# The w1_out product of a fused attention and MoE kernel by one Strassen level over groups of four token tiles, with the order of all engines written out

## The chip, the cores and the metric

One core of one Trainium2 chip. The time is the device time of one execution in microseconds (us), lower is better. Before the change three runs took 1277.09, 1277.37 and 1279.2 us; the median is 1277.37.

TensorE (PE) multiplies; "PEld" is its weight load. VectorE (DVE), ScalarE (ACT) and GpSimd (POOL) do the rest, SyncE (SP) issues the DMA transfers. SBUF is the on-chip memory, PSUM the banks that TensorE writes, DRAM the memory outside.

## The reference

Three parts follow each other for 4608 tokens of 512 numbers.

```
# attention: q, k, v of 8 batches x 8 heads x 576 tokens x 64; k and v averaged over 8 tokens each
scores = scale * q @ k_pooled.T;  attn = softmax(scores);  x = attn @ v_pooled      # x: 4608 x 512

# layer 1: w_in 512 x 1024, g_ln 1024, w_out 1024 x 512
h    = x @ w_in
solu = h * softmax(h)
ln   = (solu - mean(solu)) / sqrt(var(solu) + 1e-6) * g_ln
x    = ln @ w_out                  # the product that the change is about

# layer 2: w_in 512 x 2048, w_out 2048 x 512
h = x @ w_in;  x = (h * sigmoid(h)) @ w_out
```

## The kernel before, in words

Every product is computed to float32 accuracy from pairs of a high part and a low part: a number x is split into hi, a rounded copy, and lo = x - hi, and a product takes three matmuls (hi x hi, hi x lo, lo x hi). The splitting is work for the other engines: ScalarE copies (L181), VectorE subtracts (L182).

The 4608 tokens are 36 tiles of 128. Attention and layer 1 make up the first stage (0 to 582.49 us of the profiled execution). Per tile they run scores (`sp`, L403), softmax (L420, with GpSimd scaling the probabilities into `pb` at L429 and `lf` at L435), transposes of the probabilities (`pm` L454, `pl` L459), the product with the values (`av`, L505), the hidden product of layer 1 (`hp`, L534), its maximum (L545), the exponent (L552), the product with it (L553), a square with the sum (L562) and the scaling to the normed row on GpSimd (`e`, L568). `norm_T` transposes a normed tile (`tp`, L582) and splits it into `ln`.

`project1` multiplies by w1_out (`w1oh` and `w1ol`, scaled by g). It works on groups of two tiles (GT = 2, 256 tokens), in four chunks of 128 output columns: for each of 8 blocks of the inner dimension one 512-wide matmul (the high weights against high and low parts of `ln` side by side, L597) and one 256-wide (the low weights against the high parts, L598). ScalarE copies one half of the result (L601), VectorE adds the other (L602), and a DMA writes it to `x2d` in DRAM.

Beside this run the conversions of the weights, which lie in DRAM as pairs of 32-bit words: `tail` (L201 on ScalarE, or L205 on VectorE) and a bit join (L206). The second stage, from 582.49 us, is layer 2: its first product (L834) and its last (L1075), both by one Strassen level already.

The order of TensorE's instructions in the first stage is written by hand: SCRIPT up to tile 35, STEP and TAIL after it. A word stands for a piece (S scores, X softmax, T transposes, a or A the product with the values, H hidden product, M, E, Z the parts of the norm, N `norm_T`, P one chunk of `project1`, B a piece of the background work, W matmuls that only keep TensorE busy). `manual_schedule` holds TensorE to this order; the instructions of the other engines are put in order by a scheduler.

```
            nc.tensor.matmul(xp, wide["w1oh"][:, k, cs], ln[:, k], start=(k == 0), stop=False)
            nc.tensor.matmul(
                xp[:, :GW], wide["w1ol"][:, k, cs], ln[:, k, 0], start=False, stop=(k == FC1 - 1)
            )
        nc.scalar.activation(xo, xp[:, :GW], AF.Copy)
        nc.vector.tensor_tensor(xo, xp[:, GW:], xo, op=ALU.add)
```

## Time and profile before

| | us |
|---|---|
| runs | 1277.09, 1277.37, 1279.2 |
| span of the profiled execution | 1274.6 |
| the profiled execution's own time: its span and what lies around it (1277.37 - 1274.6 = 2.8, by the median run) | 1277.4 |
| TensorE busy | 1247.3 (98%) |
| VectorE busy | 893.1 (70%) |
| ScalarE busy | 785.8 (62%) |
| GpSimd busy | 341.7 (27%) |

The span runs from the first to the last instruction in the trace; what the execution takes beyond it lies around it. A busy share is an average over the whole span, and the two stages differ, so the rows further down are cut by stage. A row of windows has its stretch, its length, the busy us (and instruction count) of PE, PEld, DVE, ACT and POOL, the granted TensorE clock as a share of full speed, the DMA share and the GB/s moved. Each matmul line has two numbers: the busy time, in which overlapping instructions count once, and the mean duration of one, in which the pipelined part of a matmul counts too; their product is more than the busy time.

### The profile page before, as it was taken

The page shows a single profiled execution, that of the slowest core. Times are in us where ns is not written, and L with a number is a line of the kernel's source. Part 1 is how long each engine was busy: PE and PEld are TensorE (multiplying, and loading weights), DVE is VectorE, ACT ScalarE, POOL GpSimd, SP SyncE. Part 2 cuts the span into 40 slices and gives each one's busy share as a digit, 9 for nine tenths or more (in the row PEclk, how much of TensorE's full clock was granted, in tenths as well). Part 3 has the DMA queues.
Part 4 walks back from the last instruction along what each step waited for, and adds up shares of the span by engine and source line. Part 5 has one row for each costly group of instructions (what it writes and reads, how often), then busy time and mean ns, then how long its engine had stood idle before and what let it go on. Part 6 is the DMA issues. An engine that isn't in the chain of part 4 may idle for free.

```text
span 1274.6 us, 20717 instructions
## 1 busy us (share of the span) xinstructions
PE 1247.3 (98%) x6916; PEld 1124.7 (88%) x6916; DVE 893.1 (70%) x1481; ACT 785.8 (62%) x2009; POOL 341.7 (27%) x519
## 2 busy tenths in 40 slices
PE   5799999999999999999999999999999999999998
PEld 4688888888888888889999999999987888888888
DVE  6896577766765555565767676666479987969776
ACT  7975657566666566446677677667635545554544
POOL 3444344334343333332424333332040000000000
PEclk8899999999999999999999999999999999999999
DMA  8754155533533212034777697675999888777683
GB/s 295 253 188 146 54 163 167 172 123 126 171 107 124 84 62 75 26 135 144 285 288 257 242 350 284 242 247 211 366 350 395 321 285 279 268 265 259 198 294 135
DMA packets 118858, 268.76 MB, mean 211 GB/s; under 512 B 11456, under 2 KB 50368, under 8 KB 117216
## 3 DMA queue, kind: packets, MB, share of 16 engines
q1 hardware_dynamic: 118752, 267.44, 60.4%
q8 instruction: 55, 0.90, 0.3%
q14 instruction: 51, 0.42, 0.1%
HBM read 183.50 MB, written 83.89 MB: 210 GB/s over the span
## 4 chain that ended last, share of the span: by engine, by line
PE 91%; DVE 4%; ACT 3%; DMA 1%; issue 1%; POOL 0%; SPq 0%; DVEq 0%
PE m L834 27%; PE op L1075 25%; PE hp L534 14%; PE xp L597 10%; PE xp L598 5%; PE sp L403 3%; PE av L505 2%; PE tp L582 2%; PE pm L454 1%; ACT pr L420 1%; DVE gr L618 1%; DMA early<-w1i 1%; DVE gt L618 1%; PE pl L459 0%; ACT tail L201 0%
## 5 line engine op out<-in xcount | busy, mean ns | idle before, releaser
L834 PE MATMUL m<-t,w2s 128*128 128x384 f32 x2016 | 350.1, 334 | 0.0
L834 PEld LDWEIGHTS m<-t,w2s 128*128 128x128 f32 x2016 | 349.3, 188 | 0.4 <-DVE xo L602 0.3
L1075 PE MATMUL op<-gt,w2o 128*128 128x512 f32 (+1 forms) x1680 | 346.2, 368 | 0.4 <-DVE gt L618 0.3
L1075 PEld LDWEIGHTS op<-gt,w2o 128*128 128x128 f32 x1680 | 292.5, 189 | 54.1 <-DVE gt L618 2.0
L1055 ACT ACTIVATE gt<-gr 128x512 fp32r<-128x512 f32 (+1 forms) x240 | 139.8, 588 | 144.1 <-DVE gt L618 56.5
L597 PE MATMUL xp<-ln,w1oh 128*128 128x512 f32 x576 | 206.2, 399 | 0.5 <-DVE ln L182 0.4
L618 DVE TENSOR_TENSOR gt<-gr,gt 128x512 fp32r<-128x512 f32 (+1 forms) x240 | 155.1, 652 | 61.7 <-ACT gt L1055 58.3
L598 PE MATMUL xp<-ln,w1ol 128*128 128x256 f32 x576 | 161.1, 280 | 0.0
L597 PEld LDWEIGHTS xp<-ln,w1oh 128*128 128x128 f32 x576 | 108.2, 188 | 23.5 <-DVE ln L182 0.6
L534 PE MATMUL hp<-w1ih,xTh 128*128 128x512 f32 x288 | 116.5, 404 | 2.8 <-DVE e L553 2.1
L420 ACT ACTIVATE pr<-sp,st 128x72 f32<-128x72 f32 x288 | 89.3, 333 | 47.3 <-DVE st L412 46.1
L534 PE MATMUL hp<-w1ih,xTl 128*128 128x512 f32 x288 | 113.0, 392 | 0.4 <-DVE xTl L182 0.4
L534 PE MATMUL hp<-w1il,xTh 128*128 128x512 f32 x288 | 112.4, 390 | 0.0
L598 PEld LDWEIGHTS xp<-ln,w1ol 128*128 128x128 f32 x576 | 108.4, 188 | 0.4
L618 DVE TENSOR_TENSOR gr<-gr 128x512 f32<-128x512 f32 (+1 forms) x120 | 79.9, 668 | 0.2
L429 POOL TENSOR_TENSOR pb<-pr,st 128x512 f32<-128x512 f32 x36 | 38.0, 1054 | 136.8 <-DVE st L426 134.9
L545 DVE TENSOR_REDUCE ls<-hp 128x1 f32<-128x1024 f32 x36 | 44.0, 1222 | 37.5 <-PE hp L534 37.3
L618 POOL TENSOR_TENSOR tt<-x2r 128x768 f32<-128x768 f32 x22 | 43.6, 1982 | 96.4 <-DMA x2r<-x2d 67.9
L181 ACT ACTIVATE ln<-tp 128x512 fp32r<-128x512 f32 x72 | 39.6, 599 | 44.0 <-PE tp L582 43.8
L534 PEld LDWEIGHTS hp<-w1ih,xTh 128*128 128x128 f32 x288 | 54.2, 188 | 14.0 <-DVE e L553 2.7
L534 PEld LDWEIGHTS hp<-w1ih,xTl 128*128 128x128 f32 x288 | 54.0, 188 | 12.9 <-DVE xTl L182 1.0
L420 ACT ACTIVATION_READ_ACCUMULATOR pr<-sp,st 128x1 f32 x288 | 62.9, 219 | 0.0
(135 smaller groups left out, 1965.0 us busy)
## 6 DMA issues: line engine op xcount, KB each, us to landing
w2o<-wod SPq DMA_DIRECT2D x50, 768.0 KB, 6.2
x2r<-x2d SPq DMA_DIRECT2D x12, 1536.0 KB, 7.5
gd<-ga SPq DMA_DIRECT2D x96, 192.0 KB, 2.3
gd<-gb SPq DMA_DIRECT2D x48, 384.0 KB, 2.7
w2o<-wod SPq DMA_DIRECT2D x33, 512.0 KB, 6.0
gr<-gd SPq DMA_DIRECT2D x31, 512.0 KB, 7.2
wod<-wo SPq DMA_DIRECT2D x56, 256.0 KB, 2.5
gr<-gd SPq DMA_DIRECT2D x55, 256.0 KB, 5.7
```

Source lines behind the costliest of these rows:

```text
L181: nc.scalar.activation(hi, src, AF.Copy)
L403: nc.tensor.matmul(sp[done : done + n, p // 2, (p % 2) * 2 * SP : (p % 2 + 1) * 2 * SP], q[:, p, done : done + n], kbd[b % 2][:, p, :], st ...
L420: nc.scalar.activation(pr[:, g, h], sv[:, g, h], AF.Exp, bias=st[:, 0, g, h : h + 1], accum_out=st[:, 1, g, h : h + 1],)
L429: nc.gpsimd.tensor_tensor(pb, pr[:, :, :, 0:64], st[:, 0].rearrange("p a (h o) -> p a h o", o=1).to_broadcast([P, 2, 4, 64]), op=ALU.mult,)
L534: nc.tensor.matmul(hp[:, f], l, r, start=(n == 1 and m == 0), stop=(n == KC and m == 2))
L545: nc.vector.tensor_reduce(nm, hp.rearrange("p a n -> p (a n)"), axis=AX, op=ALU.max, negate=True)
L597: nc.tensor.matmul(xp, wide["w1oh"][:, k, cs], ln[:, k], start=(k == 0), stop=False)
L598: nc.tensor.matmul(xp[:, :GW], wide["w1ol"][:, k, cs], ln[:, k, 0], start=False, stop=(k == FC1 - 1))
L618: eng.tensor_tensor(dst, a, b, op=ALU.subtract)
L834: nc.tensor.matmul(to, wt[:, a, o : o + P], tk[:, b, k], start=(start and k == 0 and m == 0), stop=(k == 1 and m == 2), skip_group_check=n ...
L1055: nc.scalar.activation(ring[m][:, 0], src, AF.Copy)
L1075: nc.tensor.matmul(acc[c, x][d], w[:, l, P * d : P * d + P], t[:, r], start=(first and f == i == 0), stop=(f == NF - 1 and i == 2), skip_g ...
```

## The change

The product with w1_out is now one Strassen level over groups of four tiles (512 tokens in two halves of 256) and the two halves of the inner and output dimensions: seven products instead of eight. For each group:

- `norm_T` writes normed, transposed tiles unsplit into a ring of six (`lnr`).
- `operand1` makes the operand of one product: where it needs one, a subtraction in the ring (`lnr<-lnr`, L739 to L748), then a copy for the high part and a subtraction for the low part, into `np`.
- `project1` runs one product as 2 blocks x 4 x 3 matmuls of 256 columns (`xq`, L785), and VectorE adds the result to a running sum (L793, `xo`) that is written to DRAM.

The seven sums of weights are made once (`load_w1o`). Three of the seven blocks do not stay in SBUF: they are written to DRAM (`w1od`) and loaded again in each group (54 loads of 512 KB). The normed rows of group 0 go to DRAM (`lnd`) and are read again near the end, so groups are multiplied in the order 1 to 7, 0, 8; layer 2 reads its tokens in a matching order (TURN).

SCRIPT is written anew, now for the whole first stage and the beginning of layer 2, each word one piece of a tile's work, down to single instructions. A suffix /1, /2 or /3 puts a piece on VectorE, ScalarE or GpSimd. `manual_schedule` holds all five engines to this order. The scheduler's background list, STEP and TAIL are gone.

```
-GT = 2
+GT = 4
+HW = GT * P // 2
+TRING = 6
+LAST = (1, 2, 3, 4, 5, 6, 7, 0, 8)
+TURN = (1, 2, 3, 4, 5, 0, 0, 1, 2, 3, 4, 5)
+PRODS = {1: (L11, R11, 0), 2: (L12, R21, 1), 6: (S2, T2, 1), 5: (S1, T1, 0), 7: (S3, T3, 1), 3: (S4, R22, 0), 4: (L22, T4, 1)}
+FROM_DRAM = (L12, S1, S4)
...
-B1,-6 q0 B7,-9 B1,-6 L0,0 S0 X0 q1 L0,1 W29 L0,2 L0,3 L1,0 B1,11 L1,3 L1,1 W4 B2,-7
...
+L0,1 L0,0 W14 L0,2 k0,0 v0,0 k0,2 L0,3 q0 l0,1 L1,0 l0,1 l0,1 W29 l0,1 l0,0 l0,1 l0,2 q1
...
+    def pick(n):
+        return (nc.vector, nc.scalar, nc.gpsimd)[(flag[0] or n) - 1]
...
+    def operand1(g, n, by=0):
+        a, b = (g, 0), (g, 1)
+        slot = 2 * PRODS[n][2]
+        for p in range(2):
+            r11, r21 = normed_part(a, 0, p), normed_part(a, 1, p)
+            r12, r22 = normed_part(b, 0, p), normed_part(b, 1, p)
+            if n == 5:
+                pick(1).tensor_tensor(r12, r12, r11, op=ALU.subtract)
+                yield
...
+            x = {1: r11, 2: r21, 5: r12, 6: r12, 7: r11, 3: r22, 4: r21}[n]
+            t = wk.tile([P, 2, 2, HW], F32R, tag=f"np{slot + p}", name="np", bufs=1)
+            copy_to(t[:, :, 0], x)
+            yield
+            low_of(t[:, :, 1], x, t[:, :, 0])
+            op_t[g, n, p] = t
+            yield
...
+    def project1(g, n):
+        assert ready["w1o",] == 4
+        j = PRODS[n][0]
+        hq = gps("xq").rearrange("p (b n) -> p b n", n=HW)
+        for b in range(2):
+            w = wp_t.pop((g, j, b)) if j in FROM_DRAM else wp_t[j][:, b]
+            for k in range(4):
+                t = op_t[g, n, k // 2]
+                for i, (l, r) in enumerate(((0, 0), (0, 1), (1, 0))):
+                    nc.tensor.matmul(
+                        hq[:, b], w[:, k, l], t[:, k % 2, r],
+                        start=(b == k == i == 0), stop=(k == 3 and i == 2),
+                        skip_group_check=True,
+                    )
+            yield
...
+        def plus1(dst, src):
+            nc.vector.tensor_tensor(dst, hq, src, op=ALU.add)
+            return dst
...
-        tc.manual_schedule(engines={ET.PE})
+        tc.manual_schedule(engines={ET.PE, ET.Activation, ET.DVE, ET.Pool, ET.SP})
```

TensorE at the start of the program, before: `idle` are the matmuls that only keep it busy, `av` the product with the values.

```order
L403 MATMUL sp<-kbd_136,q 128x144 x4
L1204 MATMUL idle<-ident 128x128 x33
L403 MATMUL sp<-kbd_136,q 128x144 x4
L454 MATMUL pm<-ident,pb 128x128 x4
L459 MATMUL pl<-ident,lf 96x128 x2
L454 MATMUL pm<-ident,pb 128x128 x4
L459 MATMUL pl<-ident,lf 96x128 x2
L403 MATMUL sp<-kbd_136,q 128x144 x8
L454 MATMUL pm<-ident,pb 128x128 x4
L459 MATMUL pl<-ident,lf 96x128 x2
L505 MATMUL av<-pth,vbh_138 128x256
```

The same place after the change:

```order
L1431 MATMUL idle<-ident 128x128 x53
L494 MATMUL sp<-kbd_144,q 128x144 x8
L553 MATMUL pm<-ident,pb 128x128 x4
L559 MATMUL pl<-ident,lf 96x128 x2
L1431 MATMUL idle<-ident 128x128 x9
L494 MATMUL sp<-kbd_144,q 128x144 x4
L553 MATMUL pm<-ident,pb 128x128 x4
L559 MATMUL pl<-ident,lf 96x128 x2
L605 MATMUL av<-pth,vbh_146 128x256
```

The scores of a tile are four matmuls. The first `av` stood behind the scores of four tiles and the transposes of three; it now stands behind those of three and of two, and most of the idle matmuls stand ahead of the first scores.

TensorE where the first matmuls of `project1` stand, before (right after tile 3's hidden product):

```order
L534 MATMUL hp<-w1ih,xTh 128x512
L534 MATMUL hp<-w1il,xTh 128x512
L534 MATMUL hp<-w1ih,xTl 128x512
L597 MATMUL xp<-ln,w1oh 128x512
L598 MATMUL xp<-ln,w1ol 128x256
L597 MATMUL xp<-ln,w1oh 128x512
L598 MATMUL xp<-ln,w1ol 128x256
```

After the change the first ones, of the first product of group 1, stand beside the last hidden products of tile 11:

```order
L643 MATMUL hp<-w1ih,xTl 128x512
L494 MATMUL sp<-kbd_144,q 128x144 x4
L785 MATMUL xq<-np,w1p 128x256 x12
L605 MATMUL av<-ptl,vbh_147 128x320
L605 MATMUL av<-pth,vbl_149 128x320
L605 MATMUL av<-ptx,vls_151 128x320
L785 MATMUL xq<-np,w1p 128x256 x12
L643 MATMUL hp<-w1ih,xTh 128x512
```

So 17 of the 72 chunks of before stood ahead of tile 12's hidden product; of the 63 products of after one does, and the others follow.

VectorE in the long middle of the first stage, before: `ln` is the split of normed rows, `xo` the sum of `project1`, `tail` and `w` the conversion of layer 2's weights.

```order
L182 TENSOR_TENSOR xTl<-av,xTh 128x256 x4
L426 RECIPROCAL st<-st 128x8
L545 TENSOR_REDUCE ls<-hp 128x1
L182 TENSOR_TENSOR ln<-tp,ln 128x4x128 x2
L553 SCALAR_TENSOR_TENSOR e,ls<-hp,e 128x1024
L206 SCALAR_TENSOR_TENSOR w<-w,tail 128x512
L602 TENSOR_TENSOR xo<-xp,xo 128x256
L205 TENSOR_SCALAR tail<-raw 128x512
L206 SCALAR_TENSOR_TENSOR w<-w,tail 128x512
```

A place after the change, in the same part of the stage:

```order
L504 TENSOR_REDUCE st<-sp 128x8
L745 TENSOR_TENSOR lnr<-lnr 128x2x256
L282 CAST np<-lnr 128x2x256
L793 TENSOR_TENSOR xo<-xq,xo 128x512
L282 CAST np<-lnr 128x2x256 x2
L793 TENSOR_TENSOR xo<-xq,xo 128x512
L287 TENSOR_TENSOR np<-lnr,np 128x2x256
L282 CAST xTh<-av 128x320
L287 TENSOR_TENSOR xTl<-av,xTh 128x320
```

The splits of normed rows out of PSUM and the 256-wide sums are gone; in their place stand subtractions, copies and low parts that read SBUF (`lnr`, `np`), sums of 512 elements, and copies (`xTh`) that ScalarE did before.

## Rows read from the trace of the kernel before

**Rows 1.** Windows by stage; the columns are told in the section on the profile.
```profile
0.00:42.46 42.46, 23.62 (x132) 21.59 (x133) 28.43 (x50) 33.84 (x119) 14.33 (x29) 0.80 0.86 293
42.46:217.05 174.59, 169.94 (x1017) 147.93 (x1015) 133.83 (x246) 121.12 (x422) 76.58 (x157) 1.00 0.49 153
217.05:582.49 365.44, 365.34 (x2120) 320.73 (x2119) 227.54 (x401) 212.33 (x664) 136.13 (x260) 1.00 0.34 110
582.49:1274.60 692.11, 688.39 (x3656) 634.48 (x3654) 503.30 (x786) 418.49 (x807) 114.66 (x73) 1.00 0.77 274
```
**Rows 2.** Waits of TensorE, 0 to 100 us: total us, times, longest.
```profile
PE sp L403 <- ACT kbd L328: 7.3, 1, 7.3
PE pm L454 <- POOL pb L429: 5.7, 2, 5.5
PE sp L403 <- ACT pr L420: 5.4, 1, 5.4
```

**Rows 3.** Instructions by line and form, TensorE: busy us, mean ns | idle before.
```profile
L834 PE MATMUL m<-t,w2s 128*128 128x384 f32 x2016 | 350.1, 334 | 0.0
...
L597 PE MATMUL xp<-ln,w1oh 128*128 128x512 f32 x576 | 206.2, 399 | 0.5 <-DVE ln L182 0.4
L598 PE MATMUL xp<-ln,w1ol 128*128 128x256 f32 x576 | 161.1, 280 | 0.0
...
L1075 PE MATMUL op<-gt,w2o 128*128 128x256 f32 x336 | 40.5, 283 | 0.0
```

**Rows 4.** Timeline of TensorE around 527 us: start us, us, instruction.
```profile
527.12 0.40 PE L597 MATMUL xp<-ln,w1oh 128*128 128x512 f32 x1
527.35 0.28 PE L598 MATMUL xp<-ln,w1ol 128*128 128x256 f32 x1
...
529.55 0.39 PE L597 MATMUL xp<-ln,w1oh 128*128 128x512 f32 x1
```

**Rows 5.** Timeline at the stage marks: VectorE's first operation, tiles 0 and 12, layer 2.
```profile
4.49 1.41 DVE L323 TENSOR_REDUCE kp<-early 128x72 f32<-128x576 f32 x2 [4.49 <-DMA early<-kT]
...
42.46 0.42 PE L534 MATMUL hp<-w1ih,xTh 128*128 128x512 f32 x1
...
217.05 0.49 PE L534 MATMUL hp<-w1ih,xTh 128*128 128x512 f32 x1
...
582.49 17.70 PE L834 MATMUL m<-t,w2s 128*128 128x384 f32 x101
```

**Rows 6.** Windows, columns as in rows 1: a crowded stretch, five early us.
```profile
42.46:94.00 51.54, 47.52 (x289) 40.95 (x288) 49.24 (x87) 43.47 (x144) 28.46 (x54) 1.00 0.65 208
...
25.00:30.00 5.00, 3.76 (x14) 2.89 (x14) 4.50 (x8) 4.50 (x11) 4.75 (x8) 0.50 0.54 199
```

**Rows 7.** Instructions by line and form, VectorE, 0 to 600 us, columns as rows 3.
```profile
L182 DVE TENSOR_TENSOR ln<-tp,ln 128x512 fp32r<-128x512 f32 x72 | 46.3, 681 | 0.7 <-ACT ln L181 0.7
...
L602 DVE TENSOR_TENSOR xo<-xp,xo 128x256 f32<-128x256 f32 x72 | 30.3, 421 | 30.0 <-ACT xo L601 28.9 <-DMA x2d<-xo 0.5
...
L205 DVE TENSOR_SCALAR tail<-raw 128x512 int32<-128x512 int32 x32 | 16.7, 520 | 0.4
...
L182 DVE TENSOR_TENSOR xTl<-av,xTh 128x256 fp32r<-128x256 f32 x28 | 11.5, 423 | 13.4 <-ACT xTh L181 12.9
...
L220 DVE SCALAR_TENSOR_TENSOR w1ol<-w,g_sb,w1oh 128x512 fp32r<-128x512 f32 x8 | 6.8, 845 | 0.1
```

**Rows 8.** Single lines: duration ns min/median/max, first and last start, form.
```profile
L205 DVE TENSOR_SCALAR tail<-raw x32: 415/419/1198, 86.5 to 464.3; 128x512 int32<-128x512 int32 x32
...
L206 DVE SCALAR_TENSOR_TENSOR w<-w,tail x48: 675/686/797, 14.6 to 483.5; 128x512 int32<-128x512 int32 x48
```

**Rows 9.** Timeline around 262 us: a GpSimd scaling and a VectorE shift.
```profile
261.86 1.20 POOL L568 TENSOR_SCALAR e<-e,ls 128x1024 f32<-128x1024 f32 x1
...
262.17 1.17 DVE L205 TENSOR_SCALAR tail<-raw 128x512 int32<-128x512 int32 x1
```

**Rows 10.** The page's costliest groups: a weight load of the product.
```profile
L598 PEld LDWEIGHTS xp<-ln,w1ol 128*128 128x128 f32 x576 | 108.4, 188 | 0.4
```

More of the change, by code (lines that the diff above doesn't have):

```diff
@@ L300, in early_part @@
     def early_part(i, first, n):
+        if i == 1:
+            k = first // 1024
+            if (i, k) not in early:
+                early[i, k] = wk.tile([P, 1024], F32, tag=f"np{k}", name="early", bufs=1)
+            return early[i, k][:, first % 1024 : first % 1024 + n]
         if i not in early:
-            early[i] = wk.tile([P, 2 * FC1 * GW], F32, tag="ln", name="early")
+            early[i] = wk.tile([P, FC1 * TRING * P], F32, tag="lnr", name="early", bufs=1)
         return early[i][:, first : first + n]
@@ L395, in scores @@
         q = q_t.pop(t)
-        sp = ps.tile([P, 2, 512], F32, tag="h" if t == 1 else "s", name="sp")
+        sp = ps.tile([P, 2, 512], F32, tag="sh"[tag], name="sp")
         done = 0
@@ L509, in attend, with stat, hidden1 @@
                 m = min(n - done, RING * P - o)
-                behind["DVE"] = split(
-                    xTh[:, c, o : o + m], xTl[:, c, o : o + m], av[:, done : done + m])
+                parts.append((xTh[:, c, o : o + m], xTl[:, c, o : o + m], av[:, done : done + m]))
                 done += m
-            if c == KC - 1:
-                kept["d"] += n
+            for hi, lo, x in parts:
+                copy_to(hi, x)
             yield
-    v_t, ln_t, h_t, l_t = {}, {}, {}, {}
-    def hidden1(t, f, *part):
-        assert (t + 1) * P <= kept["d"] and kept["x"] <= (t + RING) * P
+            for hi, lo, x in parts:
+                low_of(lo, x, hi)
+            kept["d", c] = kept.get(("d", c), 0) + n
+            yield
+    def stat(t):
+        return wk.tile([P, 8], F32, tag="ls", name="ls", bufs=3)
+    v_t, h_t, l_t = {}, {}, {}
+    def hidden1(t, f, k, tag=0):
+        assert (t + 1) * P <= kept["d", k]
         if not parts.get((t, 0)) and not parts.get((t, 1)):
-            late = t > NTILE - LEAD and t % 2 == 0
-            h_t[t] = ps.tile([P, 2, 512], F32, tag="s" if late else "h", name="hp")
+            h_t[t] = ps.tile([P, 2, 512], F32, tag="hs"[tag], name="hp")
         hp = h_t[t]
@@ L584, in norm_T @@
                 )
[L585 to L606 removed]
+            yield
@@ L1293, in pooled_attention__solu__silu_kernel, with stop_attention @@
-    add(-9, ("k", 0), [prep_k(0, p) for p in range(NP)])
-    add(-8, ("v", 0), batch_v(0))
-    for f in range(2):
-        for k in range(KC):
-            add(f - 7, ("w1i", f, k), [load_w1i(f, k)])
-    lead_in(SCRIPT)
-    for a in range(FIRST, END + 1):
-        step(STEP if a < NTILE else TAIL, a, start.get(a))
-    while chunks:
-        project1(*chunks.pop(0))
+        yield
+    def stop_attention():
+        at.close()
+        open_pool("te", 1, "right")
+        open_pool("x2r", 1, "right")
+        load_tokens(0)
+        yield
+        yield from pieces(ordered(tokens(0)))
@@ new lines, in stop_hidden @@
+    def stop_hidden():
+        pi.close()
+        open_pool("wq0", 1, "right")
+        open_pool("wr", 1, "right")
+        open_pool("m", 1, "right", bt)
+        open_pool("g", 1, "right", bt)
+        load_half(0, 0)
+        yield
+        load_half(0, 1)
+        yield
+        yield from pieces(ordered(quad(0)))
+    WORDS = {
+        "q": load_q, "W": warm, "S": scores, "X": softmax, "T": probs_T, "a": attend,
+        "L": rows_w1i, "l": load_w1i, "H": hidden1, "M": solu_max, "E": solu_norm,
+        "Z": solu_scale, "N": norm_T, "u": reload_n, "R": operand1, "P": project1, "D": load_w1o_part,
+        "k": prep_k, "v": prep_v, "r": prep_v_rest, "o": load_w1o, "w": keep_f32,
+        "c": stop_attention, "d": stop_hidden, "f": first_pair,
+    }
@@ new lines, in run @@
+    def run(script):
+        words, going = script.split(), {}
+        names = [w.partition("/")[0] for w in words]
+        left = {w: names.count(w) for w in set(names)}
+        for word in words:
+            word, _, n = word.partition("/")
+            flag[0] = int(n or 0)
+            if word not in going:
+                going[word] = WORDS[word[0]](*(int(x) for x in word[1:].split(",") if x))
+            left[word] -= 1
+            next(going[word])
+            if not left[word]:
+                assert not any(True for _ in going.pop(word))
@@ L1303, in pooled_attention__solu__silu_kernel @@
+    run(SCRIPT)
+    assert kept["w"] == 32 and len(ready)
     pa.close()
```

868 lines of the change are left out of this document (476 added, 392 removed).

## The prediction

> **What bounds the kernel now.** I read the table of stages first [rows 1]. It has the span cut at three marks that the timeline gives: the first hidden product of layer 1 at 42.46 us, the first hidden product of tile 12 at 217.05, and the first product of layer 2 at 582.49 [rows 1, 5]. From 217.05 to 582.49 TensorE is busy 365.34 of 365.44 us while VectorE is busy 227.54 (62%): there only TensorE's own work counts. From 582.49 on it is busy 688.4 of 692.1, and the change does not touch that code. In the first 42.46 us it is busy 23.62, and half a stage is lost to something else. So the change can win in two ways: fewer matmul microseconds in the long stage, and an earlier start.
>
> The waits of TensorE in the first 100 us name the something else: 7.3 us for the packed keys, 5.5 of 5.7 us in one wait for the probabilities that GpSimd scales, 5.4 us for a softmax [rows 2]. Between 25 and 30 us its granted clock was 0.50 of full speed, which is the lower of its two levels [rows 6]. From 42.46 to 94 VectorE is busy 49.24 of 51.54 us, 95.5% [rows 6]: in the early tiles VectorE sets the pace, not TensorE.
>
> **The product itself.** Before, the product runs 576 pairs of a 512-wide and a 256-wide matmul [rows 3]. Seven pairs start one after another between 527.12 and 529.55 us [rows 4]: 2.43 / 7 = 0.348 us a pair, 576 x 0.348 = 200.4 us (the two busy times of the lines, 206.2 and 161.1, overlap and can't be added). Afterwards there are 9 groups x 7 products x 24 = 1512 matmuls of 256 columns. The trace has that shape in the last product of layer 2, where the weights also change with each matmul: 336 of them fill 40.5 us, 0.1205 us each [rows 3]. 1512 x 0.1205 = 182.2 us. **Term 1: -18.2 us of TensorE time.** One eighth of the multiplications goes (7 against 8 x 200.4 would be -25.1); the rest is lost again because narrower matmuls carry their fixed part more often.
>
> **What TensorE's saving costs elsewhere.** On VectorE the change removes 72 low parts of 681 ns (46.3 us), 72 additions of 421 ns (30.3), 19 shifts at 520 ns (9.9), eight scaled low parts (6.8) and five low parts of w1_in at 0.68 (3.4): 97 us [rows 7]. It adds 80 low parts, 63 additions and 39 subtractions, all over 512 elements; at the 681 ns of the nearest row that is 182 x 0.681 = 124 us. It also takes over from ScalarE and GpSimd: 12 scalings of probabilities (8 us at 681 ns), 56 copies over 512 elements (38 us at 681 ns), 68 narrower copies and low parts at 423 ns (29 us), some 22 small ones (4 us) and 8 scalings over 1024 elements (10 us at the price of two): 213 us. Net +116; 40 of the copies read and write SBUF alone, and at the 419 ns of the only such row [rows 8] they cost 10.5 us less, so +105. I take **+110 us on VectorE**. ScalarE gains about 11 us by the same counting; it has 121 of 175 and 212 of 365 us in use [rows 1], so it hides them. GpSimd gains about 86 us, on 14 + 77 + 136 = 227 in the first 582 [rows 1].
>
> The Trainium skill, VectorE: DVE Perf Modes, section The perf-mode tier table (the rule you actually need), says that a float32 copy from SBUF to SBUF runs at twice the rate of a two-input operation. The trace agrees with it on the shift, 419 against 681 ns, and has no float32 copy on VectorE; by the rule the lower end, +105, would hold.
>
> **Where this falls in time.** *Start.* The order of before puts av of the first segment behind the scores of tiles 2 and 3 and the transposes of tile 2. In the new order it comes right after the transposes of tile 1, and the warming matmuls stand ahead of the first scores instead of after them. VectorE has about 26 us of work before the first hidden product (28.4 before [rows 1]), and its first input lands at 4.49 us [rows 5]. Bounds for the first hidden product: 4.5 + 26 = 31 us if VectorE never waits, 42.5 if nothing is won. I take 36: the 5.4 us wait for the softmax goes [rows 2], and what is late next is the weights' conversion on VectorE, which nothing shortens.
>
> *To tile 12.* 17 of the 72 column chunks (136 pairs) lay before tile 12's hidden product; now one of the 63 products (24 matmuls) does. TensorE loses 46 us of work there and is no longer the pace. VectorE's work up to tile 12 is 28.43 + 133.83 = 162.3 [rows 1], by the counts 5 less; 157 - 26 leaves 131 us. Bounds: 131 at 100% busy, 154 at 85%. I take the 95.5% that the crowded stretch shows [rows 6]: 137. GpSimd takes 33 us more here than before (14 + 77 [rows 1]), under the same 137, so it is hidden. Tile 12 then begins at 36 + 137 = 173 us instead of 217.05.
>
> *From tile 12 on.* TensorE had 365.4 us here. 440 pairs go (440 x 0.348 = 153.1), 1488 matmuls come (1488 x 0.1205 = 179.3): 391.6 us. VectorE has 227.5 + 110 + 5 = 343 us in that time, 87% instead of 62%. The cover is thinner: each product now needs its operand made from four normed tiles by a subtraction, a copy and a low part, and returns its PSUM bank after an addition on VectorE that stands in a queue written out beforehand. Bounds for the stalls: 0 (GpSimd and ScalarE are given part of the pieces, and the products stand half a group behind) and 20 us, which is the 4.5% of idle time that VectorE had to keep at 95.5% [rows 6] of 392 us (18), rounded up. I take 8.
>
> The 54 reloads of weights (512 KB each) and the trip of the first group through DRAM go by SyncE's queue in a stretch where the DMA share was 0.34 [rows 1]; I cost them at nothing, hidden under matmuls of the products before. If the cover is gone, a reload is late by its own landing time, a few us, and shows at the first products of a group.
>
> **Sum.** 36 + 137 + 392 + 8 = 573 us to the start of layer 2, against 582.5: -9.5 us. Layer 2 as before (692.1): span 1265.1. The profiled execution of before had a span of 1274.6 and, with the 2.8 us around it, 1277.4, which is the median of the runs; the same 2.8 us on top give **1268 us**.
>
> **Rivals.** *A, tight packing.* The early tiles run at VectorE's 100% and the stalls vanish: 31 + 131 + 392 + 0 = 554 to 36 + 133 + 392 + 1 = 562, so 1249 to 1257. For it: TensorE's waits after 100 us are under 1 us in all in the order of before (365.34 of 365.44 [rows 1]). Against it: before, the two engines had slack against each other, now both are near full.
>
> *B, the early tiles do not shrink.* Four engines carry nearly the same load in the early tiles (about 10 us a tile each by the counts), and chains of softmax and norm cross all of them. At 85% the way to tile 12 takes 154 us: 36 + 154 + 392 + 5 = 587, +4.5 us: 1282, between 1274 and 1288. For it: TensorE had waits of 5 to 7 us while VectorE was below full [rows 2]. Against it: 95.5% was reached in just such a stretch [rows 6].
>
> *C, slower: VectorE and GpSimd get in each other's way.* A shift of VectorE over SBUF data took 1.17 us instead of 419 ns because GpSimd's scaling of e was running, and ended just after it did [rows 8, 9]. The change puts about 160 operations on VectorE that read SBUF alone (119 of them with two inputs, 40 copies) while GpSimd's load grows to about 313 of 573 us, 55%. If every one that meets GpSimd waits half a microsecond: 160 x 0.55 x 0.5 = 44 us, some 35 of them in the long stage. VectorE then needs 378 of TensorE's 392 us there, 96%, and from the 95.5% of the crowded stretch on it decides. In that stretch TensorE came to 47.52 of 51.54, 92% [rows 6]; so the long stage takes between 378 / 0.955 = 396 and 392 / 0.92 = 426, say 411, and the early one (131 + 9) / 0.955 = 147: 36 + 147 + 411 = 594, +11.5: 1289, up to 1304. Against it speaks that the 48 two-input operations over SBUF that the trace has (the bit joins of the weight conversion) run between 675 and 797 ns, median 686 [rows 8], though GpSimd is busy 77 of the 175 us of the early stage [rows 1]; only the single-input shifts reach 1198. If only the 40 copies are hit, by the 100 ns that the shift's mean lies above its median [rows 7, 8], the price is 4 us, and that is inside my 8.
>
> The Trainium skill, SBUF — State Buffer, section Who interferes with whom, states that both kinds meet GpSimd on a shared port pair that one engine locks for a whole instruction. The trace bears it out for the shift and hardly for the two-input joins; by the rule C's 44 us would hold, and the time would be C's.
>
> *D, the narrow matmuls are held by their weight loads.* At 188 ns a load [rows 10] 1512 would take 284 us, +84. The row of 0.1205 us per 256-wide matmul has its loads in it [rows 3]: excluded, about 0.
>
> **Chances.** Forecast (1260 to 1274) 0.52; A 0.13; B 0.20; C 0.15. A measurement of this kernel can tell 0.2%, 2.6 us, from no change. The forecast gives 0.48 faster and 0.04 same, A 0.13 faster, B 0.02 faster, 0.09 same and 0.09 slower, C 0.15 slower: 0.63, 0.13, 0.24. Range: A's upper half at 1254 to B's end at 1289, which leaves out A's lower half and the upper half of C; the unknown costs (start 31 to 42, early 131 to 154, stalls 0 to 20) give 1249 to over 1300 together.
>
> **What would show it.** In the new profile: the product's matmuls at about 0.12 us and 182 us in all (if more, term 1 is wrong); the first hidden product near 36 us; tile 12's near 173 with TensorE idle before it and VectorE 95% busy (190 would be B); then TensorE nearly without gaps for 392 us, its few waits on the operand parts of the products; layer 2's stage unchanged at 692. Two-input subtractions of 1 us and more, or TensorE waiting over 20 us in the long stage, would be C and make the prediction wrong; waits for reloaded weights would mean that I missed the queue.

## The result: slower, and the profile after

The changed kernel took 1292.82 us (median of 4 runs, 1290.8 to 1296.52) against 1277.23 of the kernel before beside it: ratio 1.0123, interval 1.0104 to 1.0142. It is 15.6 us slower; 9.5 us faster had been forecast. The saving of TensorE work came about as forecast, and more than that was lost between the matmuls.

Two lines of the changed kernel's page: the engines' busy totals, and TensorE's granted clock in tenths in 40 slices.

```profile
PE 1244.0 (96%) x7276; PEld 1134.2 (88%) x7276; DVE 1016.6 (79%) x1689; ACT 795.8 (62%) x1965; POOL 461.6 (36%) x623
...
PEclk8899999999999999999999999999999999999999
```

VectorE works 124 us more and GpSimd 120 us more than before; TensorE is busy 96% of its span instead of 98%. By stage, with the columns of [rows 1], cut at the first hidden products of tiles 0 and 12 and at the 49th matmul of layer 2:

```profile
0.00:38.79 38.79, 26.76 (x181) 25.07 (x182) 28.39 (x49) 25.99 (x94) 18.81 (x35) 0.91 0.87 302
38.79:186.29 147.50, 129.22 (x704) 106.78 (x704) 130.61 (x248) 123.23 (x444) 110.02 (x206) 0.95 0.76 240
186.29:593.02 406.73, 398.92 (x2746) 367.48 (x2745) 351.06 (x607) 228.10 (x623) 212.82 (x308) 1.00 0.50 163
593.02:1289.50 696.48, 689.06 (x3649) 634.92 (x3648) 506.53 (x787) 418.43 (x806) 119.92 (x76) 1.00 0.77 274
```

In the second row no engine is full: VectorE 88.5%, TensorE 87.6%, ScalarE 83.5%, GpSimd 74.6%, at a granted clock of 0.95 where before it was 1.00. VectorE's 130.61 us of work there are what had been forecast (131); it is the length that is not.

A busy time also counts the tails of pipelined matmuls, so I set TensorE's work against the clock on the wall instead: a matmul of 256 columns counts 0.1205 us and one of 384 0.1737 [rows 3], others in line with these; idle matmuls count nothing. Length less work is what a stage lost (us). The work column is thus a count at the forecast's own prices, not a second measurement of them:

| stage | before: length, work, lost | after: length, work, lost |
|---|---|---|
| to the first hidden product | 42.5, 5.5, 37.0 | 38.8, 4.7, 34.1 |
| tiles 0 to 11 | 174.6, 146.8, 27.8 | 147.5, 101.7, 45.8 |
| tiles 12 to 29 | 266.2, 246.6, 19.6 | 281.1, 257.6, 23.5 |
| tile 30 to layer 2's 49th matmul | 100.3, 97.1, 3.2 | 125.7, 113.7, 11.9 |
| layer 2's next 92 matmuls (49th to 141st) | 16.0, 16.0, 0.0 | 22.3, 16.0, 6.4 |
| sum | 599.5, 511.8, 87.7 | 615.4, 493.7, 121.7 |

The work fell by 18.1 us; the losses rose by 34.0, 18.0 of them in tiles 0 to 11. From the 141st matmul on both kernels are alike (the 141st matmul lies 15.9 us later, the last of all 15.0).

The product's lines after (columns as [rows 3]) and what TensorE waited for (total us, times, longest):

```profile
L785 PE MATMUL xq<-np,w1p 128*128 128x256 f32 x864 | 113.5, 284 | 1.3 <-DVE np L287 1.0 <-POOL np L287 0.2
...
L785 PE MATMUL xq<-np,w1o 128*128 128x256 f32 x648 | 86.7, 286 | 5.1 <-DVE np L287 3.7 <-DMA w1o<-w1od 1.4
```

```profile
PE pm L553 <- POOL pb L525: 10.5, 4, 4.6
PE xq L785 <- DVE np L287: 4.7, 4, 3.5
PE hp L643 <- DVE e L668: 4.5, 7, 1.3
PE sp L494 <- ACT pr L513: 4.0, 2, 3.8
```

The two lines of the product hold 200 us of busy time, not the 182 that the prediction looked for: a matmul lasts 284 to 286 ns in the mean, while within the product the next one starts 119 ns later (median, in e1 below as well), so each pause adds the tail of one matmul.

The waits are many and small, on all three other engines: no single one is the loss.

### The profile page after: what moved, and what is told of

Same layout as the page of the kernel before. It is cut to its first block, busy times and chain, and to the rows that moved or that the text cites. A ratio compares the mean times of both kernels' runs of the same rounds, so it can differ in the third digit from the quotient of the medians.

```text
span 1289.5 us, 21677 instructions
## 1 busy us (share of the span) xinstructions
PE 1244.0 (96%) x7276; PEld 1134.2 (88%) x7276; DVE 1016.6 (79%) x1689; ACT 795.8 (62%) x1965; POOL 461.6 (36%) x623
## 4 chain that ended last, share of the span: by engine, by line
PE 52%; DMA 1%; DVE 1%; issue 0%; ACT 0%; DVEq 0%; SPq 0%; ACTq 0%
PE op L1286 27%; PE m L1043 25%; DMA gd<-gb 1%; DMA w2r<-w2if 0%; DVE w2r L837 0%; PE xq L785 0%; DVE np L287 0%; DVE xo L793 0%; DVE gb L1054 0%; ACT gt L1266 0%; DVE t L837 0%; DVE wt L872 0%; DVE np L282 0%; DVE wt L837 0%; DVE w2s L837 0%
## 5 line engine op out<-in xcount | busy, mean ns | idle before, releaser
L643 PE MATMUL hp<-w1ih,xTh 128*128 128x512 f32 x288 | 119.6, 415 | 7.3 <-DVE e L668 4.5
L785 PE MATMUL xq<-np,w1p 128*128 128x256 f32 x864 | 113.5, 284 | 1.3 <-DVE np L287 1.0
L785 PEld LDWEIGHTS xq<-np,w1p 128*128 128x128 f32 x864 | 107.0, 189 | 3.9 <-DVE np L287 1.7
L785 PE MATMUL xq<-np,w1o 128*128 128x256 f32 x648 | 86.7, 286 | 5.1 <-DVE np L287 3.7
L785 PEld LDWEIGHTS xq<-np,w1o 128*128 128x128 f32 x648 | 81.8, 192 | 7.8 <-DVE np L287 4.1
L287 POOL TENSOR_TENSOR np<-lnr,np 128x512 fp32r<-128x512 f32 x46 | 62.2, 1356 | 49.7 <-DVE np L282 28.8
L287 DVE TENSOR_TENSOR np<-lnr,np 128x512 fp32r<-128x512 f32 x80 | 64.6, 815 | 4.4 <-ACT np L280 2.7
L666 ACT ACTIVATE e<-hp,ls 128x1024 f32<-128x1024 f32 x36 | 40.1, 1115 | 45.2 <-DVE ls L656 40.4
L280 ACT ACTIVATE np<-lnr 128x512 fp32r<-128x512 f32 x69 | 43.0, 630 | 36.1 <-PE xq L785 18.0
```

The costliest lines, as they stand in the source:

```text
L280: eng.activation(dst, src, AF.Copy)
L287: pick(1).tensor_tensor(lo, src, hi.bitcast(F32), op=ALU.subtract)
L643: nc.tensor.matmul(hp[:, f], l, r, start=(n == 1 and m == 0), stop=(n == KC and m == 2))
L666: nc.scalar.activation(e, hp, AF.Exp, bias=nm, accum_out=sm)
L785: nc.tensor.matmul(hq[:, b], w[:, k, l], t[:, k % 2, r], start=(b == k == i == 0), stop=(k == 3 and i == 2), skip_group_check=True,)
```

## The experiments

Differences are to the changed kernel's 1292.8 us unless another is named; every ratio is to the kernel before, run beside it. The changed kernel's interval is 2.4 us to either side, so a difference below that says nothing. Single profiles of an untouched stage "tiles 0 to 11" came out between 147 and 151 us, so less than 4 us there says nothing.

**Is the saving real? (e1)** `project1` of the kernel before:

```
-            nc.tensor.matmul(xp, wide["w1oh"][:, k, cs], ln[:, k], ...)
-            nc.tensor.matmul(xp[:, :GW], wide["w1ol"][:, k, cs], ln[:, k, 0], ...)
+            for l, r in (("w1oh", 0), ("w1oh", 1), ("w1ol", 0)):      # k = 0 to 6
+                nc.tensor.matmul(xp[:, :GW], wide[l][:, k, cs], ln[:, k, r], ...)
```

> The kernel before, with only its matmuls of the w1_out product changed: each of the 72 chunks runs 21 matmuls of 256 columns (hi x hi, hi x lo, lo x hi over 7 of the 8 inner blocks, all into the same 256 columns) instead of 8 pairs of 512 and 256, so 1512 in all as in the change; the last inner block is left out and VectorE adds the same half of PSUM twice, so the product's values are not the reference's. Nothing else moves. Theory 1 (the saving of TensorE time is real and is lost elsewhere): the product takes 1512 x 0.1205 = 182 us instead of 200, TensorE is busy all the time where it stands, so 16 to 19 us faster, 1258 to 1261. Rival (the narrow matmuls carry more than the 0.12 us in this place): under 6 us faster.

Measured: 1259.39 us, ratio 0.986 (0.9843 to 0.9876), 17.3 us faster than before. Theory 1 holds: the work counts as the same 493.7 us as in the change, and the losses stay (89.5 against 87.7). This run measures the saving.

**Is TensorE the pace from tile 12 on? (e2)**

```
-                for i, (l, r) in enumerate(((0, 0), (0, 1), (1, 0))):
+                for i, (l, r) in enumerate(((0, 0), (0, 1), (1, 0))[: 1 if k == 3 else 3]):
```

> The changed kernel with 20 instead of 24 matmuls in each of the 63 products (for the last of the four inner blocks only hi x hi is left, so the values are not the reference's); operands, additions, DMAs and order as they are. 252 matmuls of 0.124 us less are 31 us of TensorE time. Theory 1 (from tile 12 on TensorE still sets the pace, the loss is in the early tiles and where layer 2 starts): 22 to 31 us faster than the changed kernel, 1262 to 1271. Rival (VectorE and GpSimd, which lock each other out, have become the bound of the long stage): under 10 us faster, 1283 or more.

Measured: 1284.79, ratio 1.0066 (1.005 to 1.0082): 8 us faster, in the rival's range. Theory 1 fell as I had put it: in the profiled execution (1288.05, the slowest of the four), of 30 us less work 16 went into losses in tiles 12 to 29 (23.5 to 39.6) and 8 behind tile 30 (11.9 to 19.5). Other chains stand right behind TensorE; that VectorE and GpSimd hold each other up, as the rival says, e3 tests.

**Contention of VectorE and GpSimd? (e3)** For GpSimd's operand subtractions:

```
+        nc.gpsimd.tensor_tensor(dst[:, :, 0:2], x[:, :, 0:2], y[:, :, 0:2], op=ALU.subtract)
+        for _ in range(2):
+            nc.gpsimd.memset(dst.bitcast(F32), 0.0)
```

> The changed kernel, where GpSimd's subtractions for the operands (46 low parts and 33 differences, 1.3 to 1.4 us each in the trace) are replaced by one subtraction of two columns and two fills with zeros of the same tile, about as long together, which read nothing from SBUF but those columns; the values are not the reference's. GpSimd stays about as busy and everything waits for the same things. Theory 1 (packing, not contention): VectorE's two-input operations fall back from 815 to about 690 ns, but the time falls by less than 6 us, 1287 to 1293. Rival (contention of VectorE and GpSimd over SBUF reads made the kernel slower): 10 to 28 us faster, 1265 to 1283; 28 us is the time by which VectorE's operations of the first stage exceed their shortest more than before.

The low parts on VectorE, in the changed kernel and in this one (columns as [rows 7]):

```profile
L287 DVE TENSOR_TENSOR np<-lnr,np 128x512 fp32r<-128x512 f32 x80 | 64.6, 815 | 4.4 <-ACT np L280 2.7 <-POOL np L284 0.8
```

```profile
L734 DVE TENSOR_TENSOR np<-lnr,np 128x512 fp32r<-128x512 f32 x80 | 56.1, 708 | 5.3 <-ACT np L280 3.7 <-POOL np L284 0.8
```

Measured: 1290.72, ratio 1.011 (1.0095 to 1.0126), 2 us faster, in theory 1's range. The low parts fell from 815 to 708 ns, and VectorE's busy time from 1016.6 to 999.6 us, so the collision is real and mostly hidden. Only GpSimd's operand subtractions were taken away; its other work stayed.

**VectorE's copies on ScalarE (e4); only TensorE's order held (e5)**

```
-... R1,1/1 ... a7/1 ... T19/1 ...            # e4: 105 such pieces from tile 12 on
+... R1,1 ... a7 ... T19 ...
-        tc.manual_schedule(engines={ET.PE, ET.Activation, ET.DVE, ET.Pool, ET.SP})
+        tc.manual_schedule(engines={ET.PE})   # e5
```

> The changed kernel, with the copies that the new order gave to VectorE (high parts of operands, normed rows, probabilities, attention outputs: 105 pieces) back on ScalarE from the hidden product of tile 12 on, each at its place in the order; values unchanged. VectorE has about 50 us less, ScalarE 60 us more of the long stage. Theory 1 (TensorE sets the pace there, VectorE is short at its end only): 0 to 6 us faster, most of it where layer 2 starts, 1287 to 1293. Rival (VectorE is the bound of the long stage): over 10 us faster.

> The changed kernel with only TensorE held to the written order, as in the kernel before; ScalarE, VectorE, GpSimd and SyncE are put in order by the scheduler, with the same pieces on the same engines. Values unchanged. Theory 1 (the work itself fills VectorE and ScalarE up to tile 18, whatever its order): within 10 us of the changed kernel, 1283 to 1303, more likely slower. Rival (the written order makes engines wait in their queues for pieces that are not ready): 10 us or more faster, below 1283.

Measured: e4 1301.97, ratio 1.02 (1.0184 to 1.0215), 9 us slower, a miss for both theories: tiles 12 to 29 took 293.0 instead of 281.1, though ScalarE had room on average. e5 1377.4, ratio 1.0792 (1.0774 to 1.081), 85 us slower, far outside what I expected. The order of the other engines is worth more than any relief tried here.

**Less VectorE work (e6), with fewer matmuls (e7), with less ScalarE work (e9, e15); fillers (e8)**

```
-        nc.vector.reduce_sum(kp[:, p], raw, axis=AX)                           # e6, e7 (with e2's edit), e15; the lines of the values likewise
+        nc.vector.reduce_sum(kp[:, p], raw[:, :, 0:4] if b else raw, axis=AX)
+                nc.scalar.activation(pr[:, g], sv[:, g], AF.Exp, bias=st[:, 0, g, 0:1])   # e9, e15: t < 12
-... X5 S5 ... T10 ...
+... X5 W12,0 S5 ... W11,0 T10 ...             # e8: 15 places (second number only a name)
```

> The changed kernel, where the averages of keys and values of batches 1 to 7 add 4 of 8 rows (the values are not the reference's): VectorE's 70 reductions take about 0.36 us instead of 0.67 to 0.75, 23 us less in the first stage; nothing else changes. Theory 1 (VectorE's added work sets the pace in much of the first stage, which is why 31 us less of TensorE work gave only 8): 8 to 18 us faster than the changed kernel, 1275 to 1285. Rival (TensorE's own work and the chains between the engines set it): under 4 us faster, 1289 to 1293.

> Both edits at once: 20 of 24 matmuls in each product, and the averages over 4 of 8 rows (values not the reference's). Theory 1 (TensorE and VectorE are both near full, and each hides the other's relief): more than the two gains together, 8 + that of the half averages + at least 5 more. Rival (independent places): the sum of the two gains.

> The changed kernel with idle matmuls, 72 more in 15 places where TensorE waited 0.45 us or more between 36 and 560 us, each filling some 70% of its gap; values unchanged. The mean granted clock of the changed kernel is 0.989 of its span against 0.993 before, which is 14.2 against 8.9 us. Theory 1 (part of the loss is that the clock falls behind the new gaps): the granted clock comes back to 0.992 or so and the time falls by 2 to 6 us, 1287 to 1291. Rival (the clock costs nothing where TensorE waits anyway): within 1.5 us, or slower because the fillers are late.

> The changed kernel, where in tiles 0 to 11 the eight exponents of a tile (one per head, each with a sum read back) are two over four heads each, without sums (the values of these tiles are not the reference's): about 3.5 us of ScalarE less per tile, 42 us of the 149 us that ScalarE works up to tile 12. Theory 1 (up to tile 12 the other engines together set the pace, ScalarE's softmax chain among them, while TensorE has 102 us of work in 148): tile 12 begins 8 to 20 us earlier, and the time is 1273 to 1285. Rival (VectorE alone sets the pace there): tile 12 less than 4 us earlier, 1288 or more.

> The edits of half averages (VectorE) and of two exponents a tile up to tile 11 (ScalarE) together, values not the reference's. Alone they gave 5.6 and 1.5 us. Theory 1 (co-limited): up to tile 12 at least 6 us more than the two together, 1278 or less. Rival (VectorE's order alone): about the sum, 1285 to 1287.

Measured: e6 1287.21, ratio 1.0082 (1.0067 to 1.0097), 5.6 us faster, between its two theories; e7 1279.63, 1.0019 (1.0008 to 1.003), 13.2 us, the sum of e2 and e6 and not more; e9 1291.07, 1.012 (1.0097 to 1.0143), the rival's; e15 1289.82, 1.0098 (1.007 to 1.0125), no more than e6 alone within its spread (1285.1 to 1293.4). With the half averages tiles 0 to 11 took 142.6, 145.8 and 147.1 us in e6, e7 and e15, so even e6's gain is not certain to lie there. Co-limited engines, theory 1 of e7 and e15, fall with both. In e8 the mean clock of the runs lay between 0.994 and 0.997, against 0.988 to 0.991 in the changed kernel, and the time stayed (1293.12, 1.0119, 1.0102 to 1.0136): the lower clock cost nothing here that the run could show.

**Waits and operands by name: low parts at the end (e10), probabilities on VectorE (e11)**

```
+            if g in (0, 8):                   # e10; products of these groups read the high part twice
+                low_of(t[:, :, 1, 0:2], x[:, :, 0:2], t[:, :, 0, 0:2])
-... X10 ...                                   # e11: the scaling piece of tiles 5, 6, 10, 12, 15
+... X10/1 ...
```

> The changed kernel, where for the last two groups (0 and 8) the low part of an operand is made of two columns only and not read (the matmuls that read it read the high part instead; the values of these groups are not the reference's): the same TensorE work, some 17 us of VectorE and GpSimd less in the last 60 us of the first stage, and each operand ready one step earlier. Theory 1 (from tile 30 to the first windows of layer 2 the operands' chain and VectorE, not TensorE, set the pace; 15 us were lost there): 6 to 13 us faster than the changed kernel, 1280 to 1287. Rival (that chain is hidden, TensorE sets the pace): under 3 us faster.

> The changed kernel with the scaling of the probabilities of five tiles (5, 6, 10, 12, 15), for which TensorE waited 10.5 us in all, on VectorE instead of GpSimd; values unchanged. 0.69 us a piece there instead of 1.05 to 1.29, and not behind GpSimd's queue. If these waits are the pace (theory 2): 3 to 8 us faster. If all engines are full up to tile 12 (theory 1): within 2 us, since VectorE takes the work at its own cost.

Measured: e10 1293.41, 1.013 (1.0115 to 1.0145), unmoved: theory 1 missed, and the rival's number came, though not its reason; e11 1291.43, 1.011 (1.0093 to 1.0127), within 2 us. In e10 the wait for low parts went and one for reloaded weights took its place, 5.2 us instead of 1.4:

```profile
PE xq L788 <- DMA w1o<-w1od: 5.2, 4, 3.4
PE xq L788 <- DVE np L287: 1.3, 3, 0.7
```

In e11 the wait did not go: of 10.5 us for the probabilities 9.6 were left, half of them now on VectorE. So e11 does not show what these waits are worth.

```profile
PE pm L524 <- POOL pb L496: 4.8, 1, 4.8
PE pm L524 <- DVE pb L496: 4.8, 3, 3.1
```

**Transfers: no reloads (e12), half loads (e13), reloads by ScalarE (e14)**

```
+        if ("kept", b) not in wp_t:           # e12: one tile for all
+            wp_t["kept", b] = ...
-            nc.sync.dma_start(raw, kT[b, :, p])                                # e13; the lines of the values likewise
+            nc.sync.dma_start(raw[:, : SP // 2], kT[b, :, p][:, : SP // 2])
-        nc.vector.reduce_sum(kp[:, p], raw, axis=AX)
+        halves(kp[:, p], raw, SP)             # one reduction that reads the first half twice
-        nc.sync.dma_start(t.bitcast(F32), w1od[j][b])                          # e14
+        nc.scalar.dma_start(t.bitcast(F32), w1od[j][b])
```

> The changed kernel without the reloads of weights: one block stays in SBUF and serves all three products that would take one from DRAM (values not the reference's). 52 loads of 512 KB less, and SyncE does not wait for their buffers, which it did for 139 us in the trace. Same TensorE work. Theory 3 (transfers and SyncE's queue are what the operands and weights wait for): 6 to 14 us faster than the changed kernel, 1279 to 1287, from tile 12 on. Theory 1 (engines full, transfers hidden): within 3 us.

> The changed kernel, where the loads of keys and values of batches 1 to 7 bring half their rows, and VectorE's reductions read these twice, with as much work as before (values not the reference's): 70 loads of half the size. Theory 3 (the early tiles wait for loads; VectorE waited 8.7 us for them up to tile 12): tile 12 begins 4 to 10 us earlier. Theory 1: less than 2 us earlier.

> The changed kernel with the 54 reloads of weights issued by ScalarE instead of SyncE, at the same places of the order; values unchanged. SyncE's other loads no longer stand behind a wait for TensorE, but ScalarE's work does. If SyncE's queue is the pace: 4 to 10 us faster. If ScalarE's queue is as tight as the others: 5 to 20 us slower.

Measured: e13 1282.8, ratio 1.0049 (1.0033 to 1.0066), 10.0 us faster, as theory 3 has it; e12 1287.88, 1.0083 (1.0066 to 1.0099), 4.9 faster, between the two theories; e14 1296.94, 1.0151 (1.0136 to 1.0167), 4 slower, a little less than the 5 to 20 for a ScalarE queue as tight as the others. In e13 tiles 0 to 11 took 139.1 us, the lowest of all so far, with VectorE's work as it was. VectorE's waits there, 38 to 187 us, in the changed kernel (total, times, longest), and what was left in e13:

```profile
DVE vlp L453 <- DMA raw<-vl: 4.9, 3, 3.5
DVE vp L425 <- DMA raw<-vm: 2.0, 4, 0.6
DVE kp L393 <- DMA raw<-kT: 1.8, 3, 1.0
```

```profile
DVE vlp L383 <- DMA raw<-vl: 0.9, 2, 0.6
DVE kp L383 <- DMA raw<-kT: 0.7, 1, 0.7
```

8.7 us of waits became 1.6 (the kernel before had 4.8 in its tiles 0 to 11), and all engines closed up (windows, columns as [rows 1]):

```profile
38.08:177.20 139.12, 126.72 (x703) 104.09 (x704) 129.20 (x248) 123.22 (x444) 110.78 (x206) 0.98 0.68 214
```

VectorE is at 93%. So the transfers of keys and values are what the early tiles waited for. Why they came late the record only suggests: they land later beside more transfers. The DMA issues from 38 to 190 us (count, KB, us to landing), first before, then after:

```profile
raw<-kT SPq DMA_DIRECT2D x17, 288.0 KB, 3.4
raw<-vm SPq DMA_DIRECT2D x18, 256.0 KB, 3.7
raw<-w2i SPq DMA_DIRECT2D x7, 512.0 KB, 4.4
...
raw<-vl SPq DMA_DIRECT2D x10, 192.0 KB, 2.8
```

```profile
raw<-w2i SPq DMA_DIRECT2D x14, 512.0 KB, 5.7
raw<-kT SPq DMA_DIRECT2D x16, 288.0 KB, 3.8
raw<-vm SPq DMA_DIRECT2D x16, 256.0 KB, 4.2
...
w2if<-w SPq DMA_DIRECT2D x13, 256.0 KB, 5.2
w1od<-w1p SPq DMA_DIRECT2D x6, 512.0 KB, 4.1
lnd<-lnr SPq DMA_DIRECT2D x4, 512.0 KB, 6.0
raw<-vl SPq DMA_DIRECT2D x10, 192.0 KB, 4.3
```

36.6 MB instead of 23.5 go in these 152 us; over tiles 0 to 11, which last longer before, it is 35.4 instead of 26.6 MB. And for the reloads SyncE stood waiting (0 to 600 us; total, times, longest):

```profile
SPq L763 <- PE xq L785: 120.7, 40, 10.5
```

In e12 tiles 12 to 29 took 277.3 us instead of 281.1; in other runs that keep the reloads and TensorE's work there (e6, e9, e10, e13, e15) they took 281.4 to 283.2. Whether the reloads' bytes or SyncE's wait in front of them cost this, no run tells apart: e14 moved the wait to ScalarE.

**Is it the crowding by layer 2's weights? (e16, e17)** The pieces w0 to w31 of the order, put back evenly:

```
-... w0 ... w2 ... w1 ...                      # 24 to 300 us
+... w0 w0 w0 w0 w0 ... w1 w1 w1 w1 w1 ...     # e16: 60 to 490 us; e17: 45 to 410 us
```

> The changed kernel with the 160 pieces of layer 2's weight conversions taken out of their places in the written order and put back evenly, a block every 13.6 us from 60 us on to 490 us; all else in the old sequence, values unchanged. Before tile 12 about nine blocks instead of sixteen: 3.5 MB of loads and 1.8 MB of writes, 7 us of VectorE and 10 of ScalarE less there; the other stages take them. Theory 4 (the early tiles were crowded by this work): tile 12 begins 5 to 10 us earlier, and tiles 12 to 18 gain 2 to 4 more; 3 to 6 are given back from tile 18 on, where VectorE is at 85 to 91%: 1281 to 1288. Rival (the places were chosen right and a coarser spread only disturbs): 1293 or more.

> The same with a block every 11.5 us from 45 to 410 us: about twelve blocks before tile 12. Theory 4: between the changed kernel and the wider spread up to tile 12, 2 to 5 us earlier there, and less given back behind: 1283 to 1290. Rival: 1293 or more.

Measured: e16 1313.22, ratio 1.0291 (1.0274 to 1.0308); e17 1310.34, 1.0263 (1.0248 to 1.0279): 18 to 20 us slower, and tiles 0 to 11 took 154 us. Theory 4 was not borne out. That moving these pieces disturbs a finely fitted order more than their load costs is a reading that fits e4 and e5, but it was not tested, and so it stays open whether the added transfers of weights made the loads of keys and values late. Fewer of them in an order made anew weren't tried.

**All three transfers' places at once (e18)** e12 and e13 together, and

```
-            plan(n, tokens(1), 12, 34)
+            plan(n, tokens(1), 17, 34)
```

> The changed kernel with both edits to the transfers (half the rows of keys and values loaded, read twice; no reloads of weights; values not the reference's), and with the GpSimd subtractions for layer 2's second token block planned five slots later. The three are read from different stages: up to tile 12, tile 12 to 35, and the first windows of layer 2. Theory 3 (transfers are waited for in separate places): 13 to 17 us faster than the changed kernel from the transfers, 1276 to 1280; rival: they hide each other, under 11. For the tokens: if the collisions of VectorE and GpSimd are the price at the start of layer 2, the stretch from the 48th to the 140th matmul of layer 2 falls from 22.3 to 17 to 19 us; if it is the late weights, it stays at 21 or more.

The last edit moves all pieces of that token block, VectorE's and ScalarE's too.

Measured: 1277.87 us, ratio 1.0012 (1.0003 to 1.0022): 14.9 us faster than the change, level with the kernel before. By stage: tiles 0 to 11 139.0, tiles 12 to 29 277.4, the 92 matmuls of layer 2 18.0 instead of 22.3 (20.9 to 22.8 in the other runs but e5); tile 30 to layer 2 was unmoved (126.7). Each gain is seen in its own stage, as theory 3 has it. The medians do not add up fully: e12 and e13 alone give the 14.9, and the 3 to 4 us at layer 2's start should have come on top. At layer 2's start the timeline of VectorE (start, us, instruction) in the kernel before, the changed kernel and e18:

```profile
588.18 0.69 DVE L618 TENSOR_TENSOR w2s<-w2r,w2s 128x512 fp32r<-128x512 f32 x1 [1.58 <-ACT w2s L664]
588.78 0.69 DVE L618 TENSOR_TENSOR w2r<-w2r 128x512 f32<-128x512 f32 x1
589.39 0.95 DVE L618 TENSOR_TENSOR t<-x2r,t 128x768 fp32r<-128x768 f32 x1
```

```profile
599.00 1.90 DVE L837 TENSOR_TENSOR w2s<-w2r,w2s 128x512 fp32r<-128x512 f32 x1 [1.17 <-ACT w2s L883]
600.83 2.31 DVE L837 TENSOR_TENSOR w2r<-w2r 128x512 f32<-128x512 f32 x1
603.06 2.58 DVE L837 TENSOR_TENSOR t<-x2r,t 128x768 fp32r<-128x768 f32 x1
605.57 0.54 DVE L1054 TENSOR_TENSOR gb<-m,u 128x384 f32<-128x384 f32 x1
```

```profile
586.39 1.95 DVE L844 TENSOR_TENSOR w2s<-w2r,w2s 128x512 fp32r<-128x512 f32 x1 [1.17 <-ACT w2s L890]
588.27 2.31 DVE L844 TENSOR_TENSOR w2r<-w2r 128x512 f32<-128x512 f32 x1
590.50 0.55 DVE L1061 TENSOR_TENSOR gb<-m,u 128x384 f32<-128x384 f32 x1
```

GpSimd's token subtractions come after the first burst of layer 2's matmuls. In the kernel before that burst (first line) had 42 matmuls and stood ahead of the last chunks of `project1`, and the subtractions ran beside those chunks; in the changed kernel it has 12, and they stand beside VectorE's operations above:

```profile
560.18 7.72 PE L834 MATMUL m<-t,w2s 128*128 128x384 f32 x42
572.67 1.86 POOL L618 TENSOR_TENSOR tt<-x2r 128x768 f32<-128x768 f32 x1 [5.64 <-DMA x2r<-x2d]
574.61 1.84 POOL L618 TENSOR_TENSOR tt<-x2r,tt 128x768 f32<-128x768 f32 x1
576.40 1.85 POOL L618 TENSOR_TENSOR tt<-x2r 128x768 f32<-128x768 f32 x1
```

```profile
598.51 1.84 POOL L837 TENSOR_TENSOR tt<-x2r 128x768 f32<-128x768 f32 x1 [7.83 <-issue]
600.43 2.16 POOL L837 TENSOR_TENSOR tt<-x2r,tt 128x768 f32<-128x768 f32 x1
602.55 2.28 POOL L837 TENSOR_TENSOR tt<-x2r 128x768 f32<-128x768 f32 x1
```

Three operations that took 0.69, 0.69 and 0.95 us before took 1.90, 2.31 and 2.58 ahead of `gb`, for which TensorE waited 2.1 us. In e18 GpSimd's subtractions hardly moved (they begin 4.9 instead of 5.5 us behind the 49th matmul) and the first two operations are as slow as in the changed kernel; what moved is VectorE's third, which now stands behind `gb`, and that wait is gone. So the fall that I had tied to the end of the collisions came with one VectorE operation moved out of the way, while two of the three collisions stayed.

## Why the prediction was wrong

The span was forecast at 1265.1 us and measured at 1289.5. Of these 24.4 us, 2.8 arose before the first hidden product, 10.5 in tiles 0 to 11, 5.7 from there to the 49th matmul of layer 2, and 5.4 after it.

- **Term 1 was right.** 18.2 us of TensorE work were forecast; e1 measured 17.3. The 18.1 of the table is the same count at the same prices.
- **VectorE's net load** was forecast at 110 us and measured at 123.5 over the span. The 40 copies within SBUF took 443 ns, near the 419 of the shift, so their lower price held; the 80 low parts took 815 ns instead of 681, which is 11 us more. The Trainium skill, VectorE: DVE Perf Modes, section The perf-mode tier table (the rule you actually need), gives a float32 copy within SBUF twice the rate of a two-input operation; the trace agrees in direction, 443 against 681 ns. GpSimd's load grew by 120 us instead of 86.
- **The start** was forecast at 36 us and measured at 38.8, inside 31 to 42.5.
- **The step that failed first is "I take the 95.5% that the crowded stretch shows", 137 us to tile 12.** It took 147.5, with VectorE at 88.5%. VectorE's work there was right (131 forecast, 130.6 measured). I priced VectorE's instructions and took for granted that their data would be there; the transfers that the new order puts into those tiles (35.4 MB instead of 26.6) I did not count at all. With half the key and value loads the stage took 139.1 us (e13) and 139.0 (e18): 8.4 of the 10.5 us. That those loads are waited for is shown; that the added transfers made them late is not, since e16 and e17 did not bear it out. The term for TensorE's work that left these tiles was also off, without consequence: 136 pairs less 24 matmuls are 44 us at the prediction's own prices, not 46.
- **"I cost them at nothing"**, the reloads, failed too: they cost 4.9 us by e12. The share of 0.34 that I read is a mean and says nothing of SyncE's order, in which a reload waits for TensorE and all later loads wait behind it (120.7 us in all). Whether this order or the bytes cost the 4.9 us is open.
- **Tile 12 to the 49th matmul of layer 2**: 392 + 8, and about 1 to that matmul, were forecast, 406.7 measured. The losses there are 12.6 us more than before. About 4 are the reloads, in tiles 12 to 29. The other 8.7 lie behind tile 30, and no run took them away (e2, e10 and e18). There TensorE waited for low parts in the changed kernel and in e18, which has no reloads, and for reloads in e10, which has light low parts; both edits together weren't tried, so the cause stays open.
- **"Layer 2 as before"** failed by 6.4 us in its first windows. Its first product does not stand at 582.49 us in the kernel before, as the prediction has it: 42 of its matmuls ran ahead of the last chunks of `project1`, from 560.18 us on, and 12 do now. So GpSimd's token subtractions, which stood beside those last chunks before, now fall beside the weight sums of layer 2. Moving that token block's pieces gave 3 to 4 us back.
- **The rivals.** The time is C's (1289, up to 1304), and so are its places (147 and 411 us against 147.5 and 406.7), but that is luck: C has VectorE at 140 and 378 us of work in them, and it had 130.6 and 351.1. Taking away GpSimd's operand subtractions gave 2 us (e3), within what the runs tell apart, and at the start of layer 2 the same collision stands in a place that I hadn't looked at. The rule of the Trainium skill, SBUF — State Buffer, section Who interferes with whom, holds for single instructions (815 against 708 ns, 2.58 against 0.95 us). It still gave no 44 us. B's place was right (VectorE at 88.5% in the early tiles, between the forecast and B's 85%); its reason, chains between full engines, was not shown.

The forecast gain of 9.5 us was the difference of two large terms, with none for late data. Even without the late loads, the reloads and the wait at `gb`, in e18, the kernel is only level with the one before, so these alone do not make up the whole miss.

## What to carry to other kernels

Before a saving on the bound engine is counted, count the bytes that the new order brings into each stage and what stands in the DMA-issuing queue ahead of them, as the busy time of every engine is counted. Relieving one engine at a time can mislead where all follow one written order: halving the loads closed up every engine, while less work on any single one gave 8 us at most. Where a wait on TensorE's list is taken away, look at the list again: in e10 another had taken its place, in e11 the same wait was still there. Moving a class of pieces by rule cost 9 to 20 us here (e4, e16, e17) and leaving four engines to the scheduler 85, so the parts of such a change are hard to judge by lifting them out.

## What was not expected of the hardware

TensorE's granted clock was 0.95 in the mean in tiles 0 to 11, where TensorE was busy 129.2 of 147.5 us; before it was 1.00, with 169.9 of 174.6 us busy. With the idle matmuls of e8 (134.3 of 145.6 us busy) it was 1.00 again in these tiles, without any gain in the time. GpSimd's two-input subtraction of 512 elements took 1.36 us in the mean in the changed kernel, its fill of the same tile 0.53 (e3).
